# Stacked linear attention and a gated FFN on one core: k loaded by GpSimd with a cast into its block-diagonal tile, and loads ordered behind transposes

## Chip, core and metric

One core of a Trainium2 chip runs the whole kernel. The metric is device time in microseconds. Of a run there is one time; the median of the runs stands for the kernel, and one further execution was recorded by the hardware profiler.

## What is computed

The reference is a decayed linear attention over blocks of 64 positions, with a state that is carried along, followed by an FFN whose hidden layer is gated by its own cosine. All inputs and the output are float32.

```python
B, H, S, D = 4, 8, 768, 64          # q, k, v; lam has one value per head
rel = pos[:, None] - pos[None, :]   # positions in a block of 64
Dmask = where(rel >= 0, lam ** rel, 0)
for b in range(S // 64):
    intra = einsum('bhic,bhjc->bhij', qb, kb) * Dmask
    intra = einsum('bhij,bhjd->bhid', intra, vb)
    inter = einsum('bhid,bhde->bhie', qb * lam ** (pos + 1), kv_state)
    out[:, :, sl] = intra + inter
    kv_state = lam ** 64 * kv_state + einsum('bhsd,bhse->bhde', kb * lam ** (63 - pos), vb)
x = out.transpose(0, 2, 1, 3).reshape(3072, 512)
h = x @ w_in                        # 512 x 2048
result = (h * cos(h)) @ w_out       # 2048 x 512
```

## The kernel before

The 3072 tokens are 24 blocks of 128. A "pair" m (0 to 11) is two blocks at the same place c of two sequences b and b + 1 (`where`, line 214), so that each load and each instruction of the attention serves both. The decay is folded into q (`q_scale`) and v (`v_scale`) as powers of lam, so that the mask is a plain triangle and the state needs no scaling.

Attention of a pair (`add_attention`, line 268): q is scaled into `q_s` (line 278, POOL); v is scaled into `v_c` (line 290, POOL), and copied into the block-diagonal tile `v_bd` (line 295, DVE); k is cast from its float32 load `k_f` to bfloat16 in the block-diagonal tile `k_bd` (line 285, on ACT for pairs 0 and 1, else on POOL). A block-diagonal tile holds two heads of 64 on its diagonal and zeros beside them; the zeros are written once at the start (lines 152 to 156), whole tiles: three `k_bd` by DVE, three `v_bd` and three `kv_bd` by POOL. q_s and k_bd are transposed into `qT` and `kT`: for pairs 0 to 3 by TensorE with a copy by DVE (lines 317, 323), from pair 4 on (`DMA_FROM`) by a DMA transpose that SP issues (line 329), three to a pair. Then TensorE computes scores (line 351), DVE masks them into `s_m` (line 357), TensorE adds k times v into the running state in PSUM (`update`, line 370), DVE and ACT copy the state to `kv_bd` (line 374), TensorE makes the output from s_m, v_bd, qT and kv_bd (lines 383, 385), and ACT writes it as `xT` (line 391), which is the FFN's input, already transposed.

FFN (`add_ffn`, line 428): the blocks are grouped in tiles of 4, 2, 4, 4, 4, 4, 2 (`TILES`). For each of 16 slices of the hidden layer TensorE multiplies (`ps_h`, line 438), ACT takes the cosine (445), DVE multiplies into `g` (451). Then TensorE projects (`ps_f`, line 476), ACT copies to `o_sb` (489), and SP stores 256 KB (494).

Loads (`add_load`, line 217): SP issues everything for a pair: q as one DMA of 512 KB, and k and v as four DMAs of 128 KB each (two halves of 64 positions, each for even and odd heads, line 221). In memory a row of one head is 64 float32, 256 bytes. The weights are loaded by POOL's queue with a cast to bfloat16, eight DMAs of 512 KB (lines 255, 258; bytes counted as written). `ORDER` gives the order: pairs 0 and 1 first on SP, then w_in and w_out; the first weight waits for an early load of pair 1, and the load of pair 2 waits until the third chunk of w_out has landed.

What sets the order of everything: `Planner` (line 31) takes each step as a task with an engine, an assumed duration, dependencies and a priority, simulates, and the instructions are emitted in the order of the simulated starts. So the order on each engine is fixed when the kernel is built, and an engine waits at its next instruction until that one's semaphores are there. SP's queue holds loads, transposes and stores in one such order. The load of a pair may run ahead of it by the buffers alone: `q_f`, `k_f` and `v_f` have three each. `keep_awake` (line 532) fills TensorE's gaps before the FFN with small matmuls on a unit matrix (line 534).

Of the kernel before, what the change touches and what calls it, by code (L numbers as in the profile page):

```python
# [17 lines left out]
ORDER = "b0 b1 i0 i1 i2 i3 o0 o1 o2 o3"  # L18
DMA_FROM = 4
# [73 lines left out]
def kernel(  # L93
# [54 lines left out]
    NV, NK = 3, 3  # L148
    k_bd = [consts.tile([P, 2, 2, NP, P], BF16, name=f"k_bd{i}") for i in range(NV)]
# [34 lines left out]
    pl = Planner({**BUFS, "q_f": 3, "k_f": 3, "v_f": 3, "q_s": 2, "v_c": 3, "qT": 3, "kT": 3, "s_m": 3})  # L184
# [4 lines left out]
    for eng, us in (("SP", 1.3), ("POOL", 3.0), ("DVE", 4.6), ("ACT", 7.3)):  # L189
        pl.add(eng, us, [], None, -1e9)  # L190
# [11 lines left out]
    load_t, issue_t = {}, {}  # L202
    last_issue = {}
# [13 lines left out]
    def add_load(m, prio, deps=()):  # L217
        b, c = where(m)

        def start(o, x):  # L220
            i = nc.sync.dma_start(out=o, in_=x)  # L221
            for d in deps:
# [18 lines left out]
        for j, (name, x) in enumerate((("k_f", k), ("v_f", v))):  # L241
            for s in range(2):
                it, load_t[name, m, s] = dma("SP", 1.2, 0.8, partial(emit_kv, name, x, s), prio + 0.2 + 0.2 * j + 0.1 * s,
                                             deps, get=None if s else name)
                if s == 0:
                    issue_t[name, m] = it

    halves = [(slice(i * D, (i + 1) * D), i) for i in range(2)]
# [17 lines left out]
    Tq, Tk, qT_t, kT_t, Sc, So, V, Vo, U, Uo = ({} for _ in range(10))  # L266

    def add_attention(m):
# [3 lines left out]
        kb, vb = k_bd[m % NV], v_bd[m % NV]  # L272
        used_k = [Tk.get((m - NV, s)) for s in range(2)] + [U.get((m - NV, s)) for s in range(2)]
# [23 lines left out]
        a = pl.add("POOL", 2.1, [load_t["q_f", m], table], prep_q, pa(-0.9), get="q_s")  # L297
        issue_t["q_f", m].frees = [a]
        bk, dv, db = {}, {}, {}
        for s in range(2):  # L300
            bk[s] = pl.add("ACT" if early else "POOL", 1.24, [load_t["k_f", m, s]] + used_k,
                           partial(prep_k, s), pa(-0.85 + 0.1 * s))
# [3 lines left out]
        issue_t["k_f", m].frees = [bk[0], bk[1]]  # L306
# [266 lines left out]
```

## Time and profile before

| | us |
|---|---|
| median of 3 runs | 254.85 (252.98 to 255.15) |
| the profiled execution | 256.42 |
| its span | 254.4 |
| mean granted TensorE clock in it | 0.953 of full speed |

The span runs from the first to the last instruction in the trace; the rest of the execution's time lies around it. A granted clock of 1.0 is 2.4 GHz; the lower level is 1.2 GHz. Engines: PE is TensorE, PEld its weight loads, DVE VectorE, ACT ScalarE, POOL GpSimd, SP SyncE (SPq and POOLq are sequencers, which issue DMAs). An idle time has behind "<-" what ended it. A matmul row's time is modelled and overlaps with the next one's.

### The profile page before, as it was taken

To read this page: it belongs to the slowest core of one execution; us is meant where nothing else is said; L and a number is where in the kernel's file an instruction comes from. 1 tells how busy PE (TensorE), PEld (TensorE's weight loads), DVE (VectorE), ACT (ScalarE), POOL (GpSimd) and SP (SyncE) were. 2 spreads that over 40 slices of the span, in tenths; PEclk is the share of its full clock that TensorE was granted. 3 is DMA by queue.
4 is the path that set the end of the run, shared out by engine and by line. 5 is a ranking of instruction groups with operands and counts; after the bars stand their busy time and mean duration, and the time that the engine had idled before them with its cause. 6 is when DMAs were issued, how large, how long until landed. Compare 5 with 4: busy or idle time off the path is not lost.

```text
span 254.4 us, 4988 instructions
## 1 busy us (share of the span) xinstructions
PE 216.4 (85%) x1971; PEld 124.2 (49%) x1971; DVE 132.5 (52%) x223; ACT 120.2 (47%) x201; POOL 87.3 (34%) x102
## 2 busy tenths in 40 slices
PE   7197899879863095599959999999999999999994
PEld 7197644446641072255534455545544444465651
DVE  7266378178992046247764656565545353433220
ACT  4637478113552044057635555555554544553421
POOL 8996200976687436541836063000000000000000
PEclk9779999999999659799988999999999999999999
DMA  6999999997879989999996999809111110112112
GB/s 122 186 190 192 198 200 212 211 205 169 215 160 220 212 184 190 201 196 196 208 169 165 162 216 243 123 32 137 41 44 43 41 41 3 41 41 83 45 41 82
DMA packets 108791, 35.98 MB, mean 141 GB/s; under 512 B 101472, under 2 KB 105824, under 8 KB 108768
## 3 DMA queue, kind: packets, MB, share of 16 engines
q1 hardware_dynamic: 104400, 31.34, 60.8%
q0 software_dynamic: 4224, 4.19, 10.3%
q8 instruction: 15, 0.25, 0.4%
q10 hardware_dynamic: 144, 0.13, 0.2%
q14 instruction: 8, 0.07, 0.1%
HBM read 27.27 MB, written 6.29 MB: 132 GB/s over the span
## 4 chain that ended last, share of the span: by engine, by line
PE 59%; SPq 11%; DVE 10%; DMA 8%; POOL 6%; issue 3%; ACT 2%; POOLq 0%
PE ps_f L476 26%; PE ps_h L438 23%; SPq L221 8%; DMA v_f<-in_v_dram 5%; DVE v_bd L295 5%; SPq L329 3%; POOL v_c L290 2%; PE ps_t L317 2%; PE ps_f L438 2%; POOL v_bd L154 2%; PE ps_o L385 2%; DVE kT L323 1%; PE ps_o L383 1%; DMA kT<-k_bd 1%; PE ps_s L351 1%
## 5 line engine op out<-in xcount | busy, mean ns | idle before, releaser
L445 ACT ACTIVATE cos<-ps_h,halfpi 128x512 f32<-128x512 f32 (+1 forms) x107 | 66.3, 624 | 78.9 <-PE ps_h L438 66.0
L438 PE MATMUL ps_h<-xT,w_in_sb 128*128 128x512 bf16 (+1 forms) x428 | 97.4, 357 | 3.8 <-DVE g L451 3.1
L451 DVE TENSOR_TENSOR g<-ps_h,cos 128x512 bf16<-128x512 f32 (+1 forms) x107 | 64.8, 610 | 68.5 <-ACT cos L445 68.2
L476 PE MATMUL ps_f<-w_out_sb,g 128*128 128x512 bf16 x368 | 93.5, 382 | 1.4 <-ACT o_sb L489 0.7
L438 PEld LDWEIGHTS <-w_in_sb 128*128 128x128 bf16 x448 | 44.0, 101 | 46.7 <-issue 8.0
L476 PEld LDWEIGHTS <-g 128*128 128x128 bf16 x384 | 35.1, 98 | 34.3 <-issue 2.4
L278 POOL TENSOR_TENSOR q_s<-q_f,q_scale 128x1024 bf16<-128x1024 f32 x12 | 22.8, 1901 | 53.5 <-DMA q_f<-in_q_dram 38.9
L357 DVE TENSOR_TENSOR s_m<-ps_s,mask 128x512 bf16<-128x512 f32 x24 | 16.1, 687 | 22.5 <-PE ps_s L351 22.4
L290 POOL TENSOR_TENSOR v_c<-v_f,v_scale 128x512 bf16<-128x512 f32 x24 | 24.7, 1040 | 8.6 <-DMA v_f<-in_v_dram 7.7
L285 POOL CAST k_bd<-k_f 64x512 bf16<-64x512 f32 x40 | 24.5, 613 | 4.8 <-DMA k_f<-in_k_dram 2.8
L489 ACT COPY o_sb<-ps_f 128x512 f32<-128x512 f32 x23 | 13.5, 585 | 26.3 <-PE ps_f L476 26.2
L295 DVE COPY v_bd<-v_c 64x512 bf16<-64x512 bf16 x48 | 24.2, 505 | 0.5
L351 PE MATMUL ps_s<-qT,kT 128*128 128x64 bf16 x192 | 10.2, 203 | 16.8 <-DMA kT<-k_bd 16.7
L374 ACT CAST kv_bd<-ps_kv 64x512 bf16<-64x512 f32 x26 | 15.1, 580 | 12.7 <-PE ps_kv L370 8.5
L351 PEld LDWEIGHTS <-kT 128*128 128x128 bf16 x192 | 8.6, 104 | 21.2 <-DMA kT<-k_bd 18.2
L385 PE MATMUL ps_o<-s_m,v_bd 128*128 128x64 bf16 x192 | 16.0, 197 | 1.4 <-DVE s_m L357 1.4
L391 ACT CAST xT<-ps_o 128x512 bf16<-128x512 f32 x24 | 14.0, 581 | 4.8 <-PE ps_o L385 4.6
L383 PE MATMUL ps_o<-qT,kv_bd 128*128 128x64 bf16 x176 | 15.7, 197 | 0.2 <-ACT xT L391 0.2
L385 PEld LDWEIGHTS <-v_bd 128*128 128x128 bf16 x192 | 13.2, 101 | 4.7 <-issue 1.5
L534 PE MATMUL ps_h<-ident 128*128 128x64 bf16 x307 | 14.0, 211 | 1.6 <-POOL ident masks.py:199 1.6
L383 PEld LDWEIGHTS <-kv_bd 128*128 128x128 bf16 x176 | 13.4, 101 | 3.2 <-issue 0.6
L374 DVE CAST kv_bd<-ps_kv 64x512 bf16<-64x512 f32 x18 | 12.2, 680 | 3.0 <-PE ps_kv L370 2.4
(42 smaller groups left out, 101.5 us busy)
## 6 DMA issues: line engine op xcount, KB each, us to landing
q_f<-in_q_dram SPq DMA_DIRECT2D x12, 512.0 KB, 5.5
k_f<-in_k_dram SPq DMA_DIRECT2D x48, 128.0 KB, 3.8
v_f<-in_v_dram SPq DMA_DIRECT2D x48, 128.0 KB, 3.4
out_dram<-o_sb SPq DMA_DIRECT2D x23, 256.0 KB, 2.2
w_in_sb<-in_moe_w_in_dram POOLq DMA_DIRECT2D x4, 512.0 KB, 7.2
w_out_sb<-in_moe_w_out_dram POOLq DMA_DIRECT2D x4, 512.0 KB, 13.0
kT<-k_bd SPq DMA_TRANSPOSE x16, 4.0
qT<-q_s SPq DMA_TRANSPOSE x8, 4.2
```

The source lines that it names most:

```text
L278: nc.gpsimd.tensor_mul(t, live.pop(("q_f", m)).rearrange("t (b h) d -> t b h d", b=2), q_scale[:, c, :].unsqueeze(1).unsqueeze(3).to_broad ...
L285: (nc.scalar.copy if early else nc.gpsimd.tensor_copy)(kb[h, s, :, :, h], src[h])
L290: nc.gpsimd.tensor_mul(live["v_c", m][:, s], live["v_f", m][:, s].rearrange("t (b p) d -> t b p d", b=2), v_scale[:, 2 * c + s, :].unsquee ...
L295: nc.vector.tensor_copy(vb[h, s, :, :, h], live["v_c", m][h, s])
L351: nc.tensor.matmul(t[:, s, p, :], lhsT=live["kT", m][:, s, x, p, :], rhs=live["qT", m][:, 0, x, p, s * D:(s + 1) * D], start=True, stop=True)
L374: (nc.scalar.copy if eng == "ACT" else nc.vector.tensor_copy)(kv_bd[(2 * m + s) % NK][h, :, :, h], kv_ps[h])
L383: nc.tensor.matmul(o, lhsT=kv_bd[(2 * m + s - 1) % NK][:, x, p, :], rhs=live["qT", m][:, 0, x, p, s * D:(s + 1) * D], start=True, stop=False)
L385: nc.tensor.matmul(o, lhsT=vb[:, s, x, p, :], rhs=live["s_m", m, x][:, s * NP + p, :], start=alone, stop=True)
L438: ins = nc.tensor.matmul(t[:, :cols], lhsT=w_in_sb[:, kd, f * P:(f + 1) * P], rhs=live["xT", i][:, kd, :cols], start=(kd == 0), stop=(kd = ...
L445: nc.scalar.activation(c[:, :cols], live["h", i, f][:, :cols], AF.Sin, bias=halfpi)
L451: nc.vector.tensor_mul(live["g", i][:, f, :cols], live.pop(("h", i, f))[:, :cols], live.pop(("c", i, f))[:, :cols])
L476: nc.tensor.matmul(live["f", i, j], lhsT=live["g", i][:, f, j * P:(j + 1) * P], rhs=w_out_sb[:, f, :], start=(f == 0), stop=(f == KF - 1))
```

## The change

- k of pairs 2 to 11 (`NEARLY` = 2) is loaded by POOL's queue, with the cast to bfloat16 made by the DMA, straight into the diagonal blocks of `k_bd`: four DMAs to a pair as before, without `k_f` and without the cast on POOL. There are four `k_bd` (`NW` = 4) instead of three, since such a load waits for the transposes and the updates of pair m - 4. These DMAs stand behind the weights in POOL's queue, and carry no other dependency on the order of loads.
- k of pairs 0 and 1 is loaded by SP and cast by ACT as before.
- In the plan, the load of q of pair m + 2 (`LAG` = 2) is put behind the three DMA transposes of pair m, for m = 4 to 9. SP issues in order, so the v loads behind it follow too.
- The first weight waits for q of pair 1 (`GATE` = 3) instead of the first half of its k.
- The zeros are written only where they stay, by planned steps: all by DVE, except `v_bd` 1 and 2 by POOL.
- q_s of pairs 0 and 1 is made by DVE.
- The planner's assumed times change (v's issue 1.2 instead of 0.8 us; k's two issues on POOL 1.7 us). q was and is one transfer for both sequences.

```diff
-    NV, NK = 3, 3
+    NV, NW, NK = 3, 4, 3
-    for a, b in zip(k_bd, v_bd):
-        nc.vector.memset(a, 0.0)
-        nc.gpsimd.memset(b, 0.0)
-    for a in kv_bd:
-        nc.gpsimd.memset(a, 0.0)
+    def zero(t, eng, side):
+        for h, i in halves[side:side + 1]:
+            o = t[h, ..., (1 - i) * D:(2 - i) * D]
+            eng.memset(o.rearrange("t s b p m -> t (s b p) m") if len(t.shape) == 5 else
+                       o.rearrange("t b p m -> t (b p) m"), 0.0)
...
+        def emit_k(s):
+            for h, i in halves:
+                o = k_bd[m % NW][h, s, :, :, h].rearrange("t b p d -> t (b p) d")
+                ins = start(o, sub_block(k, s)[i], nc.gpsimd)
+            return ins
...
+        def add_k():
+            if m < NEARLY:
+                return
+            used = [Tk.get((m - NW, s)) for s in range(2)] + [U.get((m - NW, s)) for s in range(2)]
             for s in range(2):
...
+                _, load_t["k_f", m, s] = dma("POOL", 1.2, 1.7, partial(emit_k, s), prio + 0.2 + 0.1 * s, used)
...
+    for m in range(NW):
+        for name, tiles in (("k", k_bd), ("v", v_bd), ("kv", kv_bd)):
+            if m < len(tiles):
+                eng = "POOL" if name == "v" and m else "DVE"
...
-            nc.gpsimd.tensor_mul(t, live.pop(("q_f", m)).rearrange("t (b h) d -> t b h d", b=2),
+            (nc.vector if early else nc.gpsimd).tensor_mul(t, live.pop(("q_f", m)).rearrange("t (b h) d -> t b h d", b=2),
...
-                (nc.scalar.copy if early else nc.gpsimd.tensor_copy)(kb[h, s, :, :, h], src[h])
+                nc.scalar.copy(kb[h, s, :, :, h], src[h])
...
-        deps = [kept[-4 if which != "b" else -2]] if at and (names[at - 1][0] == "b") != (which == "b") else []
+        deps = [kept[-GATE if which != "b" else -2]] if at and (names[at - 1][0] == "b") != (which == "b") else []
         if which == "b":
-            add_load(n, at, deps)
-            kept += [load_t["q_f", n]] + [load_t[x, n, s] for x in ("k_f", "v_f") for s in range(2)]
+            add_k[n] = add_load(n, at, deps)
+            if n < NEARLY:
+                add_k[n]()
+            kept += [load_t["q_f", n]] + [load_t["v_f", n, s] for s in range(2)]
...
+    for m in range(DMA_FROM, NBLK // 2 - LAG):
+        issue_t["q_f", m + LAG].deps += [moved.issue for moved in (Tq[m, 0], Tk[m, 0], Tk[m, 1])]
```

## Rows read from the trace of the kernel before

**Rows 1.** Busy time by windows: start:end, length, engines, granted clock, DMA share, GB/s

```profile
29.50:60.00 30.50, 27.26 (x169) 13.09 (x169) 18.44 (x27) 13.32 (x20) 11.71 (x13) 1.00 1.09 201
60.00:79.00 19.00, 15.62 (x201) 10.77 (x199) 16.81 (x28) 10.28 (x20) 13.84 (x15) 1.00 0.83 197
79.00:88.00 9.00, 0.20 (x4) 0.12 (x4) 0.19 (x1) 0.00 (x0) 6.36 (x7) 0.80 0.91 191
88.00:104.00 16.00, 10.05 (x96) 7.08 (x95) 6.92 (x14) 5.93 (x11) 7.37 (x8) 0.79 1.06 202
104.00:137.00 33.00, 29.57 (x251) 15.36 (x250) 19.25 (x34) 16.51 (x27) 16.08 (x19) 0.90 0.99 189
137.00:250.70 113.70, 113.66 (x786) 58.58 (x784) 53.41 (x95) 57.34 (x96) 8.36 (x9) 1.00 0.40 83
```

**Rows 2.** Waits of PE, 30 to 140 us: total us, times, longest

```profile
PE ps_s L351 <- DMA kT<-k_bd: 16.7, 6, 8.8
```

**Rows 3.** Chain of waits, 76 to 90 us: start, us, what

```profile
82.27 3.30 DMA v_f<-in_v_dram
...
85.70 1.05 POOL v_c L290
```

**Rows 4.** Timeline of SP, 0 to 170 us: start, us, line, operation, times

```profile
39.08 0.37 SPq L221 DMA_DIRECT2D q_f<-in_q_dram  x1
...
74.09 0.57 SPq L221 DMA_DIRECT2D q_f<-in_q_dram  x1
...
80.26 2.64 SPq L221 DMA_DIRECT2D v_f<-in_v_dram  x4
83.07 1.33 SPq L329 DMA_TRANSPOSE qT<-q_s  x1
```

**Rows 5.** Timeline of POOL: k_bd and v_c of pair 4

```profile
63.38 2.68 POOL L285 CAST k_bd<-k_f 64x512 bf16<-64x512 f32 x4
66.14 2.04 POOL L290 TENSOR_TENSOR v_c<-v_f,v_scale 128x512 bf16<-128x512 f32 x2
```

**Rows 6.** DMA queues, 132 to 138 us, then the whole span: packets, MB, share

```profile
q1 hardware_dynamic: 4164, 1.03, 76.2%
...
q1 hardware_dynamic: 104400, 31.34, 60.8%
q0 software_dynamic: 4224, 4.19, 10.3%
```

**Rows 7.** Instructions by line: ns min/median/max; then a group (busy us, mean ns)

```profile
L255 POOL DMA_DIRECT2D w_in_sb<-in_moe_w_in_dram x4: 760/776/927, 16.5 to 23.0; - x4
L221 SPq DMA_DIRECT2D v_f<-in_v_dram x48: 595/633/1667, 5.8 to 149.7; - x48
...
L285 POOL CAST k_bd<-k_f 64x512 bf16<-64x512 f32 x40 | 24.5, 613 | 4.8 <-DMA k_f<-in_k_dram 2.8
```

**Rows 8.** Timeline of the start: start, us, engine, line, operation

```profile
1.12 0.91 DVE L153 MEMSET k_bd<- 128x1024 uint32 x1 [0.19 <-issue]
...
2.52 5.31 POOL L154 MEMSET v_bd<- 128x2048 bf16 x3
4.16 3.69 DVE L167 COPY lnl_st<-lnl 64x4 f32<-64x4 f32 x2
10.61 1.90 POOL L278 TENSOR_TENSOR q_s<-q_f,q_scale 128x1024 bf16<-128x1024 f32 x1
16.54 1.68 POOL L255 DMA_DIRECT2D w_in_sb<-in_moe_w_in_dram  x2
29.50 1.02 PE L438 MATMUL ps_h<-xT,w_in_sb 128*128 128x512 bf16 x4 [0.18 <-ACT xT L391]
```

**Rows 9.** Instructions of line 295: ns min/median/max

```profile
L295 DVE COPY v_bd<-v_c x48: 274/292/1941, 16.2 to 180.0; 64x512 bf16<-64x512 bf16 x48
```

**Rows 10.** Timeline of PE: eight matmuls of 256 columns, twice

```profile
75.95 1.03 PE L438 MATMUL ps_h<-xT,w_in_sb 128*128 128x256 bf16 x8
...
89.70 1.90 PE L438 MATMUL ps_h<-xT,w_in_sb 128*128 128x256 bf16 x8
```

More of the change, by code (lines that the diff above doesn't have):

```diff
@@ L181 @@
     kv_ps = psum.tile([P, 2, NP, D], F32, tag="ps_kv", name="ps_kv")
[L184 removed]
+    pl = Planner({**BUFS, "q_f": 3, "v_f": 3, "q_s": 2, "v_c": 3, "qT": 3, "kT": 3, "s_m": 3})
     MM = lambda cols, n=1: n * (cols / 2400.0 + 0.0025)
@@ L188 @@
     table = pl.add("SETUP", 5.6, [], None, -1e9)
-    for eng, us in (("SP", 1.3), ("POOL", 3.0), ("DVE", 4.6), ("ACT", 7.3)):
+    for eng, us in (("SP", 1.3), ("POOL", 2.2), ("DVE", 1.0), ("ACT", 7.3)):
         pl.add(eng, us, [], None, -1e9)
@@ L202 @@
     load_t, issue_t = {}, {}
+    Tq, Tk, qT_t, kT_t, Sc, So, V, Vo, U, Uo = ({} for _ in range(10))
     last_issue = {}
@@ L218, in add_load, with start @@
         b, c = where(m)
-        def start(o, x):
-            i = nc.sync.dma_start(out=o, in_=x)
-            for d in deps:
+        def start(o, x, eng=nc.sync):
+            i = eng.dma_start(out=o, in_=x)
+            for d in deps if eng is nc.sync else ():
                 tc.add_manual_dep(i.ins, getattr(d, "issue", d).ins.ins.name, mybir.DependencyInfo(
@@ L238, in emit_kv, with emit_k_early @@
             return ins
-        issue_t["q_f", m], load_t["q_f", m] = dma("SP", 2.4, 0.6, emit_q, prio, deps, get="q_f")
-        for j, (name, x) in enumerate((("k_f", k), ("v_f", v))):
-            for s in range(2):
[L243 to L248, printed above, removed]
+        def emit_k_early(s):
+            if s == 0:
+                live["k_f", m] = consts.tile([P, 2, 2 * NP, D], F32, name=f"k_f{m}")
+            for h, i in halves:
+                ins = start(live["k_f", m][h, s], sub_block(k, s)[i])
+            return ins
@@ new lines, in emit_k, with sub_block @@
+        def emit_k(s):
+            for h, i in halves:
+                o = k_bd[m % NW][h, s, :, :, h].rearrange("t b p d -> t (b p) d")
+                ins = start(o, sub_block(k, s)[i], nc.gpsimd)
+            return ins
+        def sub_block(x, s):
+            x = x[b:b + 2, :, c * P + s * D:c * P + (s + 1) * D, :]
+            return x.rearrange("b (p i) s d -> i s (b p) d", i=2)
+        issue_t["q_f", m], load_t["q_f", m] = dma("SP", 2.4, 0.6, emit_q, prio, deps, get="q_f")
+        for s in range(2 if m < NEARLY else 0):
+            _, load_t["k_f", m, s] = dma("SP", 1.2, 1.2, partial(emit_k_early, s), prio + 0.2 + 0.1 * s, deps)
@@ L264, in add_w @@
         _, w_t[which, c] = dma("POOL", 2.6, 0.9, emit, prio, deps)
-    Tq, Tk, qT_t, kT_t, Sc, So, V, Vo, U, Uo = ({} for _ in range(10))
+    zeroed = {}
+    for m in range(NW):
+        for name, tiles in (("k", k_bd), ("v", v_bd), ("kv", kv_bd)):
+            if m < len(tiles):
+                eng = "POOL" if name == "v" and m else "DVE"
+                zeroed[name, m] = [
+                    pl.add(eng, {"kv": 0.3}.get(name, 0.55) * (1.0 if eng == "DVE" else 1.6), [],
+                           partial(zero, tiles[m], nc.vector if eng == "DVE" else nc.gpsimd, side),
+                           -2000.0 if m == 0 else -1500.0 if name == "kv" else -999.5 if m == 1 else 900.0) for side in range(2)]
     def add_attention(m):
@@ L271, in add_attention @@
         pa = lambda part: prio_attn(2 * m, part)
-        kb, vb = k_bd[m % NV], v_bd[m % NV]
-        used_k = [Tk.get((m - NV, s)) for s in range(2)] + [U.get((m - NV, s)) for s in range(2)]
+        kb, vb = k_bd[m % NW], v_bd[m % NV]
         used_v = [V.get((m - NV, x, s)) for x in range(2) for s in range(2)]
@@ L295, in prep_vb @@
                 nc.vector.tensor_copy(vb[h, s, :, :, h], live["v_c", m][h, s])
-        a = pl.add("POOL", 2.1, [load_t["q_f", m], table], prep_q, pa(-0.9), get="q_s")
+        a = pl.add("DVE" if early else "POOL", 1.4 if early else 1.9, [load_t["q_f", m], table], prep_q, pa(-0.9), get="q_s")
         issue_t["q_f", m].frees = [a]
@@ L300, in add_attention @@
         for s in range(2):
-            bk[s] = pl.add("ACT" if early else "POOL", 1.24, [load_t["k_f", m, s]] + used_k,
-                           partial(prep_k, s), pa(-0.85 + 0.1 * s))
+            bk[s] = load_t["k_f", m, s]
+            if early:
+                bk[s] = pl.add("ACT", 1.24, [load_t["k_f", m, s]], partial(prep_k, s), pa(-0.85 + 0.1 * s))
+            zk, zv = zeroed.get(("k", m), []), zeroed.get(("v", m), [])
             dv[s] = pl.add("POOL", 1.05, [load_t["v_f", m, s], table], partial(prep_v, s), pa(-0.8 + 0.1 * s),
```

33 lines of the change are left out of this document (22 added, 11 removed).

## Prediction

> **What bounds the kernel now.** I read the page for the engines first, then windows cut where PE's idle time begins and ends, PE's waits, the chain of waits through the largest hole, and last the SP and POOL timelines around it. The windows [rows 1] show that from 137 us on PE has no idle time, while from 29.5 to 137 us it is idle for 3.24, 3.38, 8.80, 5.95 and 3.43 us, 24.8 us together. 16.7 us of that are scores (L351) waiting for a DMA transpose of k, 8.8 us the longest wait [rows 2]. Where that happens the granted clock is 0.80 and 0.79, so TensorE spends part of the stretch at 1.2 instead of 2.4 GHz [rows 1].
>
> Why is the transpose late? The chain through 79 to 88 us runs over SP's issues, a v load of 3.30 us, v_c on POOL (1.05 us), and then SP again [rows 3]. The transposes of pair 4 are issued at 83.07 us, behind the loads of pair 6, which SP began at 74.09 us [rows 4]. But the pair's k_bd and v_c were complete at about 66 and 68 us [rows 5]: what they waited for is their place in SP's queue, not data. SP needs (74.09 - 39.08)/4 = 8.75 us a pair for loads [rows 4]. PE's need is slower: (250.7 - 29.5 - 24.8 - about 5 for the clock, worked out below)/12 = 15.9 us a pair [rows 1]. So loading is no lasting bound; it starts late (39.08 us) and hands over in the wrong order, and PE pays until it has caught up.
>
> **Two prices for DMA.** Where only 256-byte packets of loads run, a packet costs 0.762 x 16 engines x 6 us / 4164 = 17.6 ns; the weights' packets on POOL's queue cost 0.103 x 16 x 254.4 / 4224 = 99 ns [rows 6].
>
> **1. Transposes of pair m ahead of the load of pair m+2.** This decides most. Nothing is added; on SP three transposes of some 1.3 us [rows 4] move in front of q and v of pair m+2. What they delay is a load that PE wants over 20 us later. What is queued behind a transpose that waits (for q_s or k_bd) is now the next load and the stores; each waits at most for q_s of the same pair, under 2 us.
>
> **2. k leaves SP.** For pairs 2 to 11 SP loses 40 issues of 0.633 us, taking k's issue like v's [rows 7]: 2.5 of 9.5 us a pair (0.57 + 8 x 0.633 + 3 x 1.33). The DMA engines still fetch the same 256-byte pieces. No row shows a cast packet of 256 bytes. From below 17.6 ns (a plain one of the same source size; the halved write could make it 10 to 15), from above the weights' 99 ns for eight times the bytes [rows 6]; I take 18, the nearest in size. Then a pair costs the engines 6144 x 17.6 / 16 = 6.8 us, as before: no throughput is won by the cast itself, only SP's time, and k may run ahead.
> The Trainium skill (DMA: Bandwidth & Descriptors, Issuing engines are not separate DMA queues) says the same: another issuing engine saves only the issue time. By it the sum is the one here, and the DMA term is not to be counted as a gain.
>
> **When does pair 4 arrive then?** k of pairs 2 to 5 can be issued right behind the last weight, since tiles 2 and 3 are fresh and 0 and 1 are free once pairs 0 and 1 are done. From about 39 us q and v of pairs 2 and 3 share the engines with those 8192 k packets: 16384 x 17.6 / 16 = 18 us, to 57 us; pair 4's q and v then take 4.5 us, pair 5's too, and transposes of pair 4 go out at 62 to 67 us instead of 83.07, and land some 4 us later. PE reaches their scores at about 79 us. The 8.80 us hole closes; I keep 1.0, because the scores may stand earlier in PE's order: minus 7.8. The waits for pairs 5 and 6 within 88 to 104 us and 104 to 137 us are the rest of the 16.7 us: 7.9, of which I take away 6.8; the waits on DVE's g in there stay.
>
> **3. POOL.** It loses the casts, 40 x 0.613 = 24.5 us [rows 7], and gains 40 DMA issues; a weight's issue took 0.776 us with as many pieces (512) [rows 7], so 31 us. A pair costs POOL 4 x 0.776 + 1.90 + 2.04 = 7.0 us [rows 5, 7, 8] where PE needs 15.9: covered. If an issue waits for the update of pair m-4, q_s and v_c queue behind it; that update lies two pairs back, so I take nothing, and 3 us as the bad end. From 60 to 79 us DVE's v_bd copies are stretched beside POOL's work: 274 ns at best, 1941 ns at worst [rows 9]. With the casts gone I take 1.4 of that window's 3.38 us.
> What speaks against the move: the Trainium skill (SBUF — State Buffer, SBUF: two separate sides) says that while VectorE runs a two-port copy, GpSimd can't write descriptors. That the two engines block each other the trace agrees with (lnl_st, 64x4, took 3.69 us for two copies beside POOL's memset [rows 8]). With that page's 3.1 us for a blocked DMA as the estimate, POOL would need 16.3 us a pair, about PE's pace.
>
> **4. The start.** Before, POOL zeroes v_bd (5.31 us) and kv_bd, and q_s of pair 0 begins behind that at 10.61 us [rows 8]. After, DVE zeroes only the off-diagonal halves, and takes early q_s. DVE is held by lam's chain until about 4.2 us; its copies of lnl_st no longer wait for POOL's memset. Half tiles have no row; a full tile took DVE 0.91 us [rows 8], so k_bd, v_bd and kv_bd (half as big, three) cost between 1.6 us (half the area) and 6.4 us (no faster a half than a tile); with 4, near the middle, q_s starts about 8.5 us, 2 us earlier. What works against it: weights start once q of pair 1 has landed, without its q_s ahead of them on POOL (1.90 of the 16.54 us [rows 8]), and so take engine time from v of pair 1. I take minus 2.0 for the first FFN matmul, now at 29.50 us [rows 8]; bounds plus 1.0 and minus 3.5. What is late next is v of pair 1.
>
> **5. The clock.** Eight 256-column matmuls took 1.03 us at 75.95 us and 1.90 us at 89.70 us, after the hole [rows 10]; the three stretches at the lower level (by [rows 1]: 0.21 x 2 x 16 = 6.7 us in 88 to 104, 6.6 us in 104 to 137) cost between 0.9 (what [rows 10] alone show) and 6.7 us (half of both). With PE's busy shares of these windows, 10.05/16 and 29.57/33, half of both is 5.0, and I take that back, since the holes that precede the fall go.
>
> **The sum.** 2.0 + 7.8 + 6.8 + 1.4 + 5.0 = 23.0 us. The profiled execution took 256.4 us (span 254.4, 2.0 around it), so 233.4; the median of the runs shown is 1.6 below it: **232 us**. What stays: 3.2 us of idle time in 29.5 to 60 us, some 4 us of waits for DVE and DMA, and PE's own work.
>
> **The rivals.**
> (a) *k's packets are dear; slower.* If a cast packet costs what a weight's does, 99 ns, a pair costs 2048 x 99 / 16 = 12.7 us for k, 4.5 for q and v, 3.4 for the transposes: 20.6 us against 15.9. Ten pairs from 39 us on end at 245 us, then come the last pair's work of 15.9 and the tail of 3.7 [rows 1]: near **265 us**. Place: scores and updates waiting for k_bd in the second half. It holds PE back from (15.9 - 7.9) x 16 / 2048 = 62 ns on, and loses against before from 19.5 us a pair, 91 ns. For it: no row with a cast of small pieces; against it: a weight packet carries eight times the bytes. The Trainium skill (DMA: Bandwidth & Descriptors, Specifications) puts full rate at 512 bytes and more, which these pieces miss; but so do the 17.6 ns ones.
> (b) *The wait moves to pairs 2 and 3.* If the k packets that run ahead are served first, q and v of pair 2 come up to 8192 x 17.6 / 16 = 9.0 us later, and PE waits after its first tile near 60 us: **241 us**. For it: both queues end on the same engines. Against: two queues share, and the FFN of two pairs, up to 2 x 15.9 us, keeps PE busy from 29.5 to near 60 us.
> (c) *POOL becomes the bound,* by its blocked issues as above: some 8 us given back, **240 us**. Against: weights issued beside DVE's copies took at most 0.927 us [rows 7].
> (d) *The order changes, the holes stay,* because PE's order puts the scores as much earlier as the transposes: only the start and a little clock remain, **251 us**. Against: the 16 us between 67 and 83 us.
>
> **Chances.** Forecast 0.62; (a) 0.07, (b) 0.17, (c) 0.06, (d) 0.08. Low end: start 3.5, all 16.7 us of transposes, 3 of the other idle time and 6.7 of clock give 226.5 by the profile and 225 in the median; I go to 224. High end: forecast with the bad ends of start, POOL and half the clock is 240, and (b) and (c) lie there; 246 leaves out (a), most of (d), and little else. A median can tell about 1% (2.5 us) from no change here. Faster by over 1%: the forecast, (b), (c) and half of (d), 0.89; within 1%: 0.04; slower: (a), 0.07.
>
> **What would show it.** Transposes of pair 4 on SP at 62 to 70 us and no wait over 2 us of L351 on them; granted clock near 1.0 from 60 us on; first FFN matmul at 27 to 28 us; the software queue with 20480 more packets at a price near 18 ns; POOL issues of k under 1 us. Wrong if the software queue's share rises by over a quarter, if L351 or L370 waits for k_bd's DMA in the second half, or if PE's idle time near 60 us grows.

## The result and the profile after

The changed kernel takes **239.21 us** (median of 4 runs, 238.25 to 240.16) beside 253.91 us for the kernel before: ratio 0.942 (0.9352 to 0.9487). Measured again, beside experiment 3, it took 240.22 beside 254.25 us, ratio 0.945 (0.9417 to 0.9482). Medians here are of all runs of a kernel; ratios and intervals are taken from its faster runs alone. So 14 to 15 us were won, where 23 were forecast. The profiled execution took 239.09 us; its span is 237.4 us, against 254.4.

Where did 17.0 us of span come from? First the windows of the kernel after, cut as in [rows 1] (start:end, length, busy time of PE, PEld, DVE, ACT, POOL, granted clock, DMA share, GB/s):

```profile
31.13:60.00 28.87, 26.21 (x180) 13.36 (x184) 16.86 (x27) 13.93 (x21) 15.18 (x18) 1.00 1.46 181
60.00:79.00 19.00, 15.32 (x169) 9.97 (x169) 13.03 (x23) 7.93 (x16) 12.15 (x15) 0.91 1.44 224
79.00:88.00 9.00, 7.15 (x95) 5.34 (x97) 4.83 (x12) 4.88 (x11) 5.44 (x6) 1.00 1.46 195
88.00:104.00 16.00, 14.04 (x137) 7.96 (x140) 11.17 (x23) 8.91 (x15) 8.05 (x9) 1.00 1.25 187
104.00:137.00 33.00, 31.15 (x260) 16.17 (x262) 23.27 (x41) 19.82 (x33) 19.80 (x18) 1.00 1.33 203
137.00:233.70 96.70, 95.95 (x639) 49.89 (x650) 41.90 (x74) 47.48 (x80) 3.90 (x3) 1.00 0.29 69
```

and the first FFN matmul:

```profile
31.13 1.89 PE L479 MATMUL ps_h<-xT,w_in_sb 128*128 128x512 bf16 x7 [0.18 <-ACT xT L432]
```

Length less PE's busy time is PE's idle time: 2.66, 3.68, 1.85, 1.96, 1.85 and 0.75 us, 12.8 us together where [rows 1] give 24.8. The hole of 8.80 us between 79 and 88 us shrank to 1.85, while 60 to 79 us has slightly more idle time than before (3.38). PE's busy time from the first FFN matmul to its last end fell from 196.4 us (the sum of [rows 1]) to 189.8, with the granted clock at 1.00 but for one window. Most of that is the clock: where it was granted at 0.50, PE was busy for 12.6 us before (84.34 to 94.58, 104.82 to 108.23 and 132.13 to 135.54 us) and for 3.2 us after (67.70 to 71.12 us); if half of such time is lost, which is an estimate, 4.7 of the 6.6 us are the clock's, and 1.9 us stay unexplained. Against that, the first FFN matmul came later, at 31.13 instead of 29.50 us. The account of the span: 12.0 (idle time) + 6.6 (busy time) - 1.6 (start) = 17.0.

PE's waits of 0.5 us and more, 31 to 140 us (total, times, longest), answer to [rows 2]:

```profile
PE ps_h L479 <- DVE g L492: 4.2, 7, 2.0
PE ps_s L392 <- DVE kT L364: 2.0, 1, 2.0
PE ps_s L392 <- DMA qT<-q_s: 1.7, 2, 1.1
PE ps_t L358 <- POOL q_s L318: 1.4, 2, 0.8
PE ps_f L517 <- DVE g L492: 0.6, 1, 0.6
PE ps_s L392 <- DMA kT<-k_bd: 0.5, 1, 0.5
```

Of 16.7 us behind a DMA transpose 2.2 are left, and the longest wait on one is 1.1 instead of 8.8 us. The largest item is now DVE's `g`, 4.2 instead of 3.1 us. The second longest single wait, 2.0 us, ends with DVE's copy of `kT` of pair 3 (DVE first, then PE):

```profile
63.30 3.27 DVE L335 COPY v_bd<-v_c 64x512 bf16<-64x512 bf16 x2 [0.60 <-POOL v_c L330]
66.61 0.69 DVE L364 COPY kT<-ps_t 128x1024 bf16<-128x1024 bf16 x1
```

```profile
67.36 0.56 PE L392 MATMUL ps_s<-qT,kT 128*128 128x64 bf16 x12 [1.99 <-DVE kT L364]
```

Two copies into `v_bd`, 0.29 us each in the median, took 3.27 us here, while POOL ran v_c and q_s, and the copy of `kT` stood behind them.

SP's timeline answers to [rows 4]:

```profile
39.11 0.37 SPq L228 DMA_DIRECT2D q_f<-in_q_dram  x1
39.52 7.44 SPq L228 DMA_DIRECT2D v_f<-in_v_dram  x4
...
48.40 9.26 SPq L228 DMA_DIRECT2D v_f<-in_v_dram  x4
...
62.88 0.58 SPq L228 DMA_DIRECT2D q_f<-in_q_dram  x1
63.57 6.03 SPq L228 DMA_DIRECT2D v_f<-in_v_dram  x4
...
71.82 1.34 SPq L370 DMA_TRANSPOSE kT<-k_bd  x1
```

The transposes of pair 4 go out at 71.82 us instead of 83.07, ahead of pair 6's load. But SP didn't get the room that was expected: four issues of v, 2.5 us by [rows 7], took 7.44 and 9.26 us, and pair 5's load still stands ahead of those transposes.

That stretch in the queues, 40 to 57 us (packets, MB, share of 16 engines), first after, then before:

```profile
DMA packets 15946, 3.02 MB, mean 178 GB/s; under 512 B 15888, under 2 KB 15943, under 8 KB 15943
...
q0 software_dynamic: 8438, 1.10, 99.1%
q1 hardware_dynamic: 7505, 1.89, 72.9%
```

```profile
DMA packets 12926, 3.57 MB, mean 210 GB/s; under 512 B 12684, under 2 KB 12796, under 8 KB 12924
...
q1 hardware_dynamic: 12796, 3.43, 101.0%
```

A cast packet's record lasts 0.991 x 16 x 17 / 8438 = 31.9 ns, and a plain one's now 0.729 x 16 x 17 / 7505 = 26.4 ns. But the shares add up to 1.72: packets of the two queues overlap in time. Per packet served, the 16 engines took 16 x 17 / 15946 = 17.1 ns; before, with almost none but plain packets, it was 16 x 17 / 12926 = 21.0 ns. So the cast isn't dear; SP's queue got 7505 packets of the engines' work in this stretch instead of 12796, and its issues waited.

POOL, in the order of time:

```profile
31.75 0.68 POOL L228 DMA_DIRECT2D k_bd<-in_k_dram  x1 [1.27 <-DMA w_in_sb<-in_moe_w_in_dram]
34.33 0.68 POOL L228 DMA_DIRECT2D k_bd<-in_k_dram  x1 [1.90 <-DMA w_out_sb<-in_moe_w_out_dram]
...
42.13 4.75 POOL L228 DMA_DIRECT2D k_bd<-in_k_dram  x7 [2.08 <-DMA w_out_sb<-in_moe_w_out_dram]
...
49.62 1.91 POOL L318 TENSOR_TENSOR q_s<-q_f,q_scale 128x1024 bf16<-128x1024 f32 x1
```

An issue takes 0.68 us, where 0.776 was forecast, but five of k's issues wait, 1.27 to 2.08 us each, by the trace until an older weight transfer has landed. POOL stood there until 49 us, with q_s of pair 2 behind it.

The start on DVE, beside [rows 8] (each row runs from the first to the last of its instructions):

```profile
5.81 1.12 DVE L160 MEMSET k_bd<- 64x512 uint32 x2
7.07 1.11 DVE L160 MEMSET v_bd<- 64x512 uint32 x2
8.28 2.08 DVE L160 MEMSET kv_bd<- 64x256 uint32 x6
10.50 1.74 DVE L160 MEMSET k_bd<- 64x512 uint32 x3
12.17 1.53 DVE L318 TENSOR_TENSOR q_s<-q_f,q_scale 128x1024 bf16<-128x1024 f32 x1
```

The two halves of a tile cost 0.97 us (1.1 with the gap between them), no less than the whole tile did (0.91 us), and q_s of pair 0 came at 12.17 us instead of 10.61.

The software queue over the whole span, beside [rows 6]:

```profile
q0 software_dynamic: 25344, 6.82, 28.4%
```

### The profile page after: what moved, and what is told of

Read it like the earlier page. It is cut to its first block, busy times and chain, and to the rows that moved or that the text cites. A ratio compares the mean times of both kernels' runs of the same rounds, so it can differ in the third digit from the quotient of the medians.

```text
span 237.4 us, 4933 instructions
## 1 busy us (share of the span) xinstructions
PE 210.1 (89%) x1943; PEld 121.9 (51%) x1972; DVE 132.8 (56%) x238; ACT 119.8 (50%) x201; POOL 83.0 (35%) x98
## 3 DMA queue, kind: packets, MB, share of 16 engines
q0 software_dynamic: 25344, 6.82, 28.4%
## 5 line engine op out<-in xcount | busy, mean ns | idle before, releaser
L479 PE MATMUL ps_h<-xT,w_in_sb 128*128 128x512 bf16 (+1 forms) x417 | 93.0, 346 | 4.9 <-DVE g L492 4.2
L517 PE MATMUL ps_f<-w_out_sb,g 128*128 128x512 bf16 x351 | 91.8, 384 | 2.1 <-DVE g L492 0.6
L479 PEld LDWEIGHTS <-w_in_sb 128*128 128x128 bf16 x448 | 43.0, 98 | 45.6 <-issue 5.5
L228 POOL DMA_DIRECT2D k_bd<-in_k_dram x40 | 27.5, 698 | 32.6 <-DMA w_out_sb<-in_moe_w_out_dram 7.7
L330 POOL TENSOR_TENSOR v_c<-v_f,v_scale 128x512 bf16<-128x512 f32 x24 | 25.5, 1081 | 12.0 <-DMA v_f<-in_v_dram 11.5
L318 POOL TENSOR_TENSOR q_s<-q_f,q_scale 128x1024 bf16<-128x1024 f32 x10 | 19.1, 1914 | 15.6 <-issue 13.2
L335 DVE COPY v_bd<-v_c 64x512 bf16<-64x512 bf16 x48 | 20.5, 428 | 1.3 <-POOL v_c L330 0.8
L426 PEld LDWEIGHTS <-v_bd 128*128 128x128 bf16 x192 | 12.4, 98 | 4.5 <-issue 1.7
L424 PEld LDWEIGHTS <-kv_bd 128*128 128x128 bf16 x176 | 12.8, 98 | 3.0 <-issue 0.5
L580 PEld LDWEIGHTS <-ident 128*128 128x128 bf16 x308 | 12.9, 111 | 1.6 <-POOL ident masks.py:199 1.6
L392 PE MATMUL ps_s<-qT,kT 128*128 128x64 bf16 x192 | 9.0, 193 | 4.9 <-DVE kT L364 2.7
```

Of the source, the lines that this page charges most:

```text
L228: i = eng.dma_start(out=o, in_=x)
L318: (nc.vector if early else nc.gpsimd).tensor_mul(t, live.pop(("q_f", m)).rearrange("t (b h) d -> t b h d", b=2), q_scale[:, c, :].unsqueez ...
L330: nc.gpsimd.tensor_mul(live["v_c", m][:, s], live["v_f", m][:, s].rearrange("t (b p) d -> t b p d", b=2), v_scale[:, 2 * c + s, :].unsquee ...
L335: nc.vector.tensor_copy(vb[h, s, :, :, h], live["v_c", m][h, s])
L424: nc.tensor.matmul(o, lhsT=kv_bd[(2 * m + s - 1) % NK][:, x, p, :], rhs=live["qT", m][:, 0, x, p, s * D:(s + 1) * D], start=True, stop=False)
L426: nc.tensor.matmul(o, lhsT=vb[:, s, x, p, :], rhs=live["s_m", m, x][:, s * NP + p, :], start=alone, stop=True)
```

## The experiments

**1. Undo the hold** (changed kernel; only SP's order differs).

```diff
-    for m in range(DMA_FROM, NBLK // 2 - LAG):
-        issue_t["q_f", m + LAG].deps += [moved.issue for moved in (Tq[m, 0], Tk[m, 0], Tk[m, 1])]
```

> The changed kernel without the hold of loads behind transposes. The order of instructions differs on SP alone, in two places: the load of pair 6 (q and v) goes ahead of the transposes of pair 4, and the load of pair 11 ahead of a store and the transposes before it. Theory (the order on SP is what decides): the transposes of pair 4 go out some 5 us later, at about 77 us, land at 82, and scores of pair 4 wait 3 to 4 us; with the clock's fall 242 to 245 us. Rival (with k off SP the queue has room, and the order no longer matters): 238 to 240.5 us, no wait over 2 us on L390's scores.

Measured: 251.1 us (246.94 to 253.24), ratio 0.9751 (0.9645 to 0.9857). By the median 3.5 us of the gain are left, by the ratio 6: between 8 and 12 us are gone. SP's timeline and PE's longest wait:

```profile
68.59 0.45 SPq L228 DMA_DIRECT2D q_f<-in_q_dram  x1
...
73.22 2.67 SPq L228 DMA_DIRECT2D v_f<-in_v_dram  x4
76.07 1.52 SPq L370 DMA_TRANSPOSE kT<-k_bd  x1
```

```profile
81.00 0.37 PE L392 MATMUL ps_s<-qT,kT 128*128 128x64 bf16 x4 [5.83 <-DMA qT<-q_s]
```

With k off SP, pair 6's load comes earlier, and so do the transposes behind it, but PE still waits 5.83 us. Since the start and k's path are as in the changed kernel, the loss is the order's. It is larger than both theories had it; the trace shows 5.8 us of it here, a clock of 0.62 in 79 to 88 us behind that hole, and 7.4 us of waits for `g` instead of 4.2.

**2. The hold alone** (kernel before, with the same two lines and `LAG = 2` added).

> The kernel before with the hold alone: k by SP, the old start, the old zeros. The order differs on SP alone. Theory (order decides): the transposes of pair 4 go out at 75 us instead of 83, the 8.8 us hole shrinks to 1 to 3 us, 242 to 247 us. Rival (the move of k brings most, since without it SP's load of the next pairs only comes later and the hole moves to pair 5 or 6): 249 to 254 us.

Measured: 242.55 us, ratio 0.9513 (0.9451 to 0.9575), 12.0 us below the kernel before. Two lines that change the order of SP's queue alone give most of the gain; the transposes of pair 4 go out 8.7 us earlier:

```profile
74.35 1.37 SPq L330 DMA_TRANSPOSE qT<-q_s  x1
```

**3. k's move alone undone** (changed kernel with the hold; k of pairs 2 to 11 by SP in float32 into three buffers and cast by POOL). With it, the changed kernel again, on the same chip.

```diff
-NEARLY = 2
+NEARLY = 12
...
+            if m < NEARLY:
+                bk[s] = pl.add("ACT" if early else "POOL", 1.24 if early else 1.3, [load_t["k_f", m, s]] + used_k,
+                               partial(prep_k, s), pa(-0.85 + 0.1 * s))
```

> The changed kernel with k's move alone undone: k of pairs 2 to 11 is loaded by SP in float32 into a buffer of three and cast by POOL, as before; the order of transposes, the zeros, early q_s on DVE and the planner's times stay. Theory A (k's move is worth about 3 us, the difference between the kernel with the hold alone, 242.55, and the changed one, 239.21): 242 to 244 us, since SP is again held by 40 issues and pair 4's transposes go out near 74 to 76 us. Theory B (k's move is worth nothing, since a cast packet takes 32 ns of an engine instead of 17.6 and gives back in the DMA engines what SP saves; the difference came from the start's edits): 238 to 240.5 us. Theory C (worth more, the start having cost 1.6 us of it): 244.5 to 246 us.

> The changed kernel as it is, measured beside the next two on the same chip, since differences of 1 to 3 us between earlier kernels are near what their intervals tell apart. 238.5 to 240.5 us.

Measured: 243.23 us, ratio 0.9542 (0.9497 to 0.9587), beside 240.22 us, ratio 0.945 (0.9417 to 0.9482). Theory A: k's move is worth 3.0 us. The windows of the kernel with k on SP, then of the changed kernel:

```profile
60.00:79.00 19.00, 14.53 (x173) 9.64 (x170) 14.39 (x25) 8.89 (x18) 13.28 (x15) 0.87 0.93 208
79.00:88.00 9.00, 7.85 (x75) 5.50 (x76) 3.74 (x8) 3.57 (x8) 3.78 (x5) 0.70 0.98 198
```

```profile
60.00:79.00 19.00, 14.55 (x176) 10.05 (x176) 13.02 (x23) 8.22 (x17) 12.19 (x16) 1.00 1.37 215
79.00:88.00 9.00, 7.55 (x84) 5.80 (x85) 4.79 (x11) 4.39 (x9) 5.91 (x6) 0.81 1.48 193
```

PE is busy for about as long in both, but at a clock of 0.87 and 0.70 instead of 1.00 and 0.81. The two profiled executions took 241.28 and 240.04 us, so their whole times differ by less than the medians; but the FFN of the first began at 30.85 us and that of the second at 32.78. From the first FFN matmul to PE's last it is 205.05 against 201.82 us, and 2.4 us of these 3.2 are busy time, 0.9 idle time. In these executions the difference shows mostly as clock. Which part of k's move brings it, SP's issues or POOL's casts, wasn't separated.

**4. k not ahead** (changed kernel; k of pair m is issued only behind v_c of pair m - 2 on POOL).

```diff
+            used += [Dv.get((m - 2, 1))]
...
+            Dv[m, s] = dv[s]
```

> The changed kernel, where k of pair m is issued on POOL only behind v_c of pair m-2, so that k of pairs 4 and 5 no longer runs ahead of q and v of pairs 2 and 3. Theory (the k that runs ahead took the engines from q and v of pairs 2 and 3, whose v_c came 3 to 4 us later than before the change): v_c of pair 2 ends by 52 instead of 55.3 us, PE's waits between 50 and 68 us (about 3.5 us) and the lower clock around 70 us go: 235 to 237.5 us. Rival (PE was not short of pairs 2 and 3, and k of pair 4 now comes too late for its transposes): 239 to 243 us.

Measured: 240.15 us, ratio 0.9432 (0.9372 to 0.9491), as the changed kernel. On POOL:

```profile
48.40 1.90 POOL L319 TENSOR_TENSOR q_s<-q_f,q_scale 128x1024 bf16<-128x1024 f32 x1 [5.49 <-DMA q_f<-in_q_dram]
```

Eight issues fewer stand ahead of q_s of pair 2, and it comes only 1.2 us earlier, since q itself has just landed. SP's issues do get room by it: pair 3's four of v take 5.11 instead of 9.26 us, and the transposes of pair 4 go out at 68.34 us. But that k runs ahead neither wins nor costs anything that can be measured in the time.

**5. k of pairs 2 and 3 on SP** (as 3, with `NEARLY = 4`).

> The changed kernel, but k of pairs 2 and 3 still by SP in float32 with the cast on POOL; k of pairs 4 to 11 by POOL's queue with the cast in the DMA. Theory (until about 57 us the DMA engines are full, and 4096 cast packets at 32 instead of 17.6 ns cost 3.7 us of them, while POOL stands at 12 issues until 49 us): q_s of pair 2 on POOL at 44 to 46 us instead of 49.62, v_c of pair 3 done by 60 us instead of 64.3, less idle time of PE in 60 to 88 us: 236 to 238.5 us. Rival (PE has enough work until pair 3 comes, or SP's 16 more issues give the time back at pair 4): 239 to 242 us.

Measured: 244.57 us, ratio 0.9617 (0.9577 to 0.9657): the theory fell, and so did the rival, which expected less of a loss. The profiled execution is the fastest of its eight (240.3 us, the others 242.9 to 245.4), so its trace doesn't show what the others lost. In it q_s of pair 2 comes at 47.79 us and v_c of pair 3 ends at 67.2 us, not by 60: the casts of pair 3 stand behind k's issues, which wait for updates. Its mean granted clock was 0.986, that of the seven others 0.951 to 0.970, so at least part of the 4 us by which the usual execution is slower is the clock; what made it fall there stays open.

**6. The weights later** (changed kernel, `GATE = 3` to `GATE = 1`: the first weight waits for the last v of pair 1).

> The changed kernel with GATE = 1: the first weight waits for the last v of pair 1 instead of its q. Theory (the start became later because the weights' packets delayed v of pair 1, whose scaling began at 25.14 instead of 21.25 us): v of pair 1 is scaled by 21 us, the first FFN matmul goes at 27 to 28.5 instead of 31.13 us, and the time is 235.5 to 237.5 us. Rival (the DMA engines bound the start, what is early there is late behind): first FFN matmul as above, but loads of pair 2 come 2 to 3 us later and the time stays at 238 to 240.5 us. Second rival (DVE's zeros delayed the start): first matmul stays at 30 us or later.

Measured: 248.22 us (242.57 to 251.34); no interval. Pair 1's v was scaled by 20.7 us instead of 26.2, as the theory said, and no earlier start came of it:

```profile
31.76 1.89 PE L479 MATMUL ps_h<-xT,w_in_sb 128*128 128x512 bf16 x7
```

```profile
43.05 0.37 SPq L228 DMA_DIRECT2D q_f<-in_q_dram  x1
```

The FFN starts no earlier, and pair 2's load, which waits for w_out, starts 3.9 us later. An earlier v of pair 1 alone doesn't bring the start forward; the second rival's sign came, though not its reason, as experiment 7 shows.

**7. The start, in four ways** (changed kernel each time): q_s of pairs 0 and 1 back on POOL; the zeros that are needed later behind q_s of pair 0; the whole old start; the first two together.

```diff
-            (nc.vector if early else nc.gpsimd).tensor_mul(
+            nc.gpsimd.tensor_mul(
```

```diff
-    for eng, us in (("SP", 1.3), ("POOL", 2.2), ("DVE", 1.0), ("ACT", 7.3)):
+    for eng, us in (("SP", 1.3), ("POOL", 2.2), ("DVE", 5.8), ("ACT", 7.3)):
...
-                           -2000.0 if m == 0 else -1500.0 if name == "kv" else -999.5 if m == 1 else 900.0) for side in range(2)]
+                           -2000.0 if m == 0 else -999.45 if name == "kv" else -999.5 if m == 1 else 900.0) for side in range(2)]
```

```diff
+    for t in k_bd:
+        nc.vector.memset(t, 0.0)
+    for t in v_bd + kv_bd:
+        nc.gpsimd.memset(t, 0.0)
...
+        deps = [load_t["k_f", 1, 0] if which != "b" else kept[-2]] if at and (names[at - 1][0] == "b") != (which == "b") else []
```

> The changed kernel with one thing undone: q_s of pairs 0 and 1 is made by POOL again, not by DVE. Theory (the later start comes from DVE's queue, in which q_s of pair 0 stood behind the zeros at 12.17 us and q_s of pair 1 at 21.03 us): POOL makes q_s of pair 0 at 6.5 to 7.5 us, the first FFN matmul comes at 28 to 29.5 us instead of 31.13, and the time falls by 1.5 to 3 us, to 236 to 237.7 us. The weights again stand behind q_s of pair 1 on POOL, so the second half of v_c of pair 1 should come near 21 to 22 us instead of 25.14. Rival (the start is set by the loads of pair 1 and PE's own chain, DVE only fills): first FFN matmul at 31 us or later, 238.5 to 240 us.

> The changed kernel with early q_s still on DVE, but the zeros that are needed later (k_bd 1 to 3, kv_bd 1 and 2) planned behind q_s of pair 0. Theory (zeros ahead of q_s cost the start): q_s of pair 0 at 8.5 to 9.5 us instead of 12.17; but q_s of pair 1 stays on DVE and v of pair 1 still lands late behind the weights' packets, so only part comes back: first FFN matmul 29.8 to 31 us, 237.5 to 239 us. Rival (the zeros only move to other gaps of the same full queue): first FFN matmul within 0.3 us of 31.13, 239 to 240 us.

> The changed kernel with the whole start of before: whole tiles zeroed at once, by DVE and POOL as before, q_s of pairs 0 and 1 on POOL, the first weight behind the first half of k of pair 1. What is left of the change is the hold and k's move to POOL. Theory (the start lost 1.6 us and nothing else hangs on it): first FFN matmul at 29.3 to 29.8 us, 237 to 238.2 us, and against the kernel with the hold alone (242.55) the move of k is worth 4.5 to 5.5 us. Rival (k's move is worth 3.3 us as the difference of the medians says, the start being paid back later): 239 to 240.5 us.

> Both edits at once: early q_s on POOL, and the zeros that are needed later behind DVE's early copies. Theory: q_s of pair 0 at 6.5 to 7.5 us, its transposed copy by DVE before 10 us, first FFN matmul at 26.5 to 28 us, which the prediction had put there for the change itself; 234.5 to 236.5 us. Rival (loads of pair 1 set the start: v of pair 1 could be scaled near 21 us at the earliest before, and 8 us follow it): first FFN matmul 28.5 to 29.5 us, 236.5 to 238 us, no better than undoing q_s alone.

Measured: 241.56 us, ratio 0.948 (0.9397 to 0.9563); 242.52, 0.9515 (0.9429 to 0.9601); 242.84, 0.9525 (0.9444 to 0.9605); 244.34, 0.9581 (0.9492 to 0.967). None is faster than the changed kernel, and the theories behind all four fell. In the first of them, POOL and then PE:

```profile
6.53 1.90 POOL L318 TENSOR_TENSOR q_s<-q_f,q_scale 128x1024 bf16<-128x1024 f32 x1
...
19.85 1.05 POOL L330 TENSOR_TENSOR v_c<-v_f,v_scale 128x512 bf16<-128x512 f32 x1
```

```profile
31.02 0.20 PE L580 MATMUL ps_h<-ident 128*128 128x64 bf16 x1 [1.23 <-issue]
31.06 1.89 PE L479 MATMUL ps_h<-xT,w_in_sb 128*128 128x512 bf16 x7
```

q_s of pair 0 comes at 6.53 instead of 12.17 us and the last v_c of pair 1 at 19.85 instead of 25.14, and the FFN starts at 31.06: within 0.1 us of the changed kernel. With the old start it starts at 31.25 us, not at 29.50. With the zeros late, q_s of pair 0 comes at 9.94 us, but v_c of pair 1 only at 29.66, and the FFN at 38.26 (in an execution of 245.62 us); with both edits it starts at 30.75 us. So neither DVE's zeros nor q_s on DVE sets it by itself. The paths differ, too. With q_s on POOL and with the old start, PE makes the second block's output, for which it waits for `xT`, before it transposes q_s of pair 1 (at 21.82 and 22.30 us); with the hold alone it transposes first (21.47 us), and its FFN starts at 29.55. That order is the planner's, from its new assumed times. In the changed kernel PE has the old order, but q_s of pair 1 leaves DVE only at 22.25 us. The first of the four stood a further 1.23 us at a filler matmul for nothing that the profile names. A kernel with PE's old order and q_s on POOL wasn't tried.

One execution says little of the start, though. Five profiles have the same program up to there: two of the changed kernel and those of experiments 1, 4 and 8. Their first FFN matmuls come at 31.13, 32.78, 30.65, 32.11 and 33.92 us, and the last v_c of pair 1 begins at 25.14, 27.56, 24.34, 26.89 and 27.89 us. In the three late ones PE stands before the state's update and waits for that v_c, 1.55, 1.28 and 2.41 us; the second profile of the changed kernel shows it:

```profile
28.64 0.39 PE L411 MATMUL ps_kv<-v_c,k_bd 128*128 128x64 bf16 x8 [1.55 <-POOL v_c L330]
```

So v of pair 1, which lands while the weights' packets run, does set the start when it comes late, and the FFN follows 5.2 to 6.0 us behind it. When it comes early (24.34 and 25.14 us here, 19.85 in the first of the four), something else holds the start at about 31 us.

The third of the four leaves of the change the hold and k's move, and takes 242.84 us; the hold alone took 242.55 (ratios 0.9525 and 0.9513). So k's move, worth 3.0 us with the new start (experiment 3), is worth nothing that shows with the old one, whose FFN under the planner's new order starts 1.7 us later than with the hold alone.

What the start is worth, though, can be read elsewhere. In the second profile of the changed kernel:

```profile
32.78 1.89 PE L479 MATMUL ps_h<-xT,w_in_sb 128*128 128x512 bf16 x8 [0.18 <-ACT xT L432]
```

That execution took 240.04 us against 239.09: the FFN began 1.65 us later, and the time is 0.95 us longer. `kT` of pair 3 is copied at 66.89 us there and at 66.61 in the first, so a PE that is later waits less for it (1.7 against 2.0 us).

**8. The hold one pair tighter** (changed kernel, `LAG = 2` to `LAG = 1`).

> The changed kernel with the hold one pair tighter (LAG = 1): the load of pair m + 1, not m + 2, stands behind the transposes of pair m. In SP's order this moves one thing of weight: q and v of pair 5 (62.88 to 69.6 us) go behind the transposes of pair 4 (71.82 us). Theory (a transpose should stand before every load that is not needed earlier): transposes of pair 4 at 66 to 69 us, no wait of PE for their DMA; but that wait is only 2.2 us now, so at best 237.5 to 239 us. Rival (pair 5's load, some 5 us later, is itself needed at 88 to 95 us, and the distance of two pairs was right): waits for pair 5 and 6 grow by 2 us or more, 241 to 244 us.

Measured: **236.78 us**, ratio 0.9295 (0.9231 to 0.9359), whose interval just touches that of the changed kernel's first measurement (from 0.9352). Its slowest run (237.46) lies below the changed kernel's fastest (238.25), though they were not measured side by side: this beats both kernels. SP's timeline, the windows, and PE's first FFN matmul:

```profile
66.16 1.33 SPq L370 DMA_TRANSPOSE kT<-k_bd  x1
...
69.05 3.06 SPq L370 DMA_TRANSPOSE kT<-k_bd  x1
...
72.80 0.41 SPq L228 DMA_DIRECT2D q_f<-in_q_dram  x1
```

```profile
60.00:79.00 19.00, 17.67 (x246) 12.81 (x247) 15.24 (x31) 10.72 (x21) 13.32 (x17) 1.00 1.40 197
```

```profile
33.92 1.89 PE L479 MATMUL ps_h<-xT,w_in_sb 128*128 128x512 bf16 x8
```

The transposes of pair 4 go out at 66.16 us, ahead of pair 5's load, PE has no wait of 0.2 us or more for a DMA transpose from 31 to 140 us, and its idle time in 60 to 79 us is 1.33 instead of 3.68 us. The FFN began at 33.92 us, later than in any other kernel here, and the time is the shortest. From the first FFN matmul to the span's end it takes 234.9 - 33.92 = 201.0 us, against 206.3 for the changed kernel and 224.9 for the one before. The rival fell: pair 5's load, ten microseconds later, is not missed. Not all of the 5.3 us are the order's: gone are the 2.2 us of waits for transposes, but also the 2.0 for `kT` of pair 3 (copied at 66.62 us here too, but PE, which began later, comes to it later) and the 1.4 for q_s of pairs 2 and 3. The later start, 2.8 us, is about paid back by these last two.

## Why the prediction was right, and where it was not

The sign, the range and the first reason were right; the size was 7.2 us too good (232.0 against 239.2). In the span it is 6.0 us: the start 3.6, the idle time 4.0, less 1.6 for PE's busy time, which the prediction took for the clock. Nearly all the rest is the 1.6 us between execution and median, which the changed kernel's profiled execution, lying on its median, doesn't have.

**Step 1 (order): right, and worth more than all the rest.** The transposes waited for their place in SP's queue: 12.0 us come with the hold alone, and 8 to 12 go when it alone is undone. The 8.8 us wait went, as the 7.8 of the sum had it (8.80 to 1.85 us of idle time).

**Step 2 (k leaves SP): the packet's price was right, the date was wrong.** A served packet costs 17.1 ns; rival (a) is dead, and [rows 6]' 99 ns belonged to longer packets. By the record's length, the measure that the prediction used, a cast packet has 31.9 ns and not 18; that overstates it, since records overlap. The Trainium skill (DMA: Bandwidth & Descriptors, Issuing engines are not separate DMA queues) had it that another issuing engine saves only the issue time, and the 17.1 ns agree. But the text took SP's issue at its median, 0.633 us, when issues stretch while the queues are full and the engines are shared with 8438 cast packets: pair 4's transposes were put at 62 to 67 us and went at 71.82. Its own figures held the sign: SP took 8.75 us a pair for loads, where the medians make only 0.57 + 8 x 0.633 = 5.6 (its sum with the transposes is 9.6 and not 9.5), and issues of k in the kernel before took up to 3.76 us. Pair 5's load stood in front of them, a second case of step 1 that the prediction passed over. Experiment 8 takes it away and finds 2.4 to 3.4 us. k's move itself is worth 3.0 us beside the new start (experiment 3) and nothing that shows beside the old one (experiment 7).

**Idle time: 16.0 us forecast to go, 12.0 went.** 79 to 88 us gave 7.0 of 7.8; 88 to 137 us gave 5.6 of 6.8; 60 to 79 us, put at 1.4, gave -0.3. The 1.4 were to come from DVE's v_bd copies, which no longer meet POOL's casts. They did shrink in that window, from 7.20 to 5.00 us together, but two of pair 3 took 3.27 us beside v_c and q_s, and PE waited 1.99 us for the copy of `kT` behind them. Rival (b), the wait that moves to pairs 2 and 3, happened in small: v_c of pair 3 began at 62.20 us, and PE waited 1.4 us for q_s of the two pairs. Its price in the time isn't shown; experiment 4, which brings q_s of pair 3 forward to 55.71 us, has the same time.

**Step 3 (POOL): the issues were right, its queue was not.** 677 to 813 ns an issue against 776 taken. What stood behind the wait was asked for updates of pair m - 4, not for the weights: 8.9 us of waiting behind them. It decides nothing here: in experiment 4 POOL itself waits 5.49 us for q of pair 2. The Trainium skill (SBUF — State Buffer, SBUF: two separate sides) names a 3.1 us blocked DMA; no issue of k took over 0.82 us, with DVE busy for 56% of the span. Whether an issue ever met such a copy isn't shown. The two engines did meet, the other way round: one of DVE's v_bd copies took 2.97 us beside POOL's v_c, where the median is 0.29. Rival (c) is dead.

**Step 4 (the start): wrong, +1.6 instead of -2.0.** Three terms were mis-sized. DVE's chain for lam held it until 5.81 us, not 4.2. The zeros were counted as one k_bd, one v_bd and three kv_bd, which took 3.6 us (four halves at 0.485, six at 0.272) where 4 were taken; but three halves of later k_bd stood ahead of q_s too, so that all of it, with gaps, held q_s for 6.4 us. And q_s of pair 1 was put into DVE's chain at no cost. But the step failed deeper: three of the four kernels that mend these terms begin their FFN at 30.75 to 31.25 us, inside the spread of the changed kernel's own start (30.65 to 33.92), and the fourth at 38.26. The text's own remark that v of pair 1 is late next holds for the late starts (experiment 7) and is not the whole cause, since bringing v forward alone doesn't help (experiment 6). And starting later doesn't cost as much later: q_s and `kT` of pairs 2 and 3 come when they come, and a late FFN waits less for them.

**Step 5 (the clock): right in size.** PE's busy time fell by 6.6 us, of which the clock makes an estimated 4.7, where 5.0 were forecast. The granted clock is 1.00 but for 0.91 in 60 to 79 us, and in experiment 3 most of what k's move wins shows as clock.

Of the signs that were to show it, these came: no wait over 2 us for pair 4's transposes, the packets (25344 - 4224 = 21120 more, where 20480 were forecast), POOL's issues under 1 us, the software queue's share up by 18.1 points and not by 25. Three did not: the date of the transposes, the first FFN matmul, and a clock near 1.0 from 60 us on (0.91 to 79 us). One sign of being wrong came faintly: the idle time in 60 to 79 us grew, by 0.3 us.

What stays open: whether the start's edits are worth something (the old start lies 2.6 us above the changed kernel, with intervals that overlap), what sets the first FFN matmul when v of pair 1 is early, why k's move pays beside one start and not beside the other, and why k of pairs 2 and 3 on SP is slower than the changed kernel and no faster than all of k on SP.

## What to carry to other kernels

Where one queue issues loads, stores and transposes, look for the transfer that is ready but stands behind one that isn't needed yet: two lines of order gave 12 of 14 us here, and one digit more gave 2.4 to 3.4. Before you pay for an earlier start, ask what the work then waits for; time saved ahead of a wait that ends at the same moment anyway is given back. One profile of a start is one draw: compare it with the spread of the same program before you explain a microsecond. Moving an issue to another engine doesn't move the bytes, and the two queues take packets from each other: cost it by packets served per engine, not by a record's length or a queue's share.

## What the runs showed of the hardware

- Packets of two queues overlap in the records: 31.9 and 26.4 ns long, yet 17.1 ns of engine time for each served. A share above 1.0 (1.72 of two queues, 1.01 of one alone before) is no mistake of the profile.
- A DMA issue on POOL can wait for an older transfer of its queue: five of k's issues waited 1.27 to 2.08 us each, by the trace for a chunk of the weights to land, though the buffer was free. Whether the queue holds them or a semaphore of the program isn't shown.
- SP's issues stretch as well: the same v issue takes 0.636 us in the median and up to 5.4 us while both queues are full; k's took up to 3.76 us in the kernel before, with SP's queue alone.
- DVE's memsets took time by the columns and not by the partitions: 0.272 us for 64 x 256, 0.485 for 64 x 512, 0.91 for 128 x 1024. The two instructions that zero half of a tile won nothing over one for the whole.
- Copies of 64 x 512 by DVE, 0.29 us in the median, took up to 2.97 us while POOL ran v_c, and 2.0 us of that reached PE.
- The first FFN matmul of one and the same program came between 30.65 and 33.92 us in five executions; in the three late ones PE waited for a load that lands beside the weights.
